# Two-layer token mixer after bucketed attention: where weight residues are subtracted, and the order in which inputs are split and read

## The chip, the core and the metric

The kernel runs on one core of a Trainium2 chip. The metric is the device time of one execution in microseconds (us), the median of several runs. TensorE (PE) multiplies matrices into PSUM; VectorE (DVE), ScalarE (ACT) and GpSimd (POOL) work element by element; SyncE (SP) starts the transfers. Each engine takes its instructions in a fixed order and waits on semaphores for those of the others.

## What is computed

An attention in which a query sees only the keys of its own hash bucket, then two feed-forward layers without bias, all in float32:

```python
def reference(q, k, v, proj, moe_w_in, moe_w_out, moe2_w_in, moe2_w_out):
    x = attn(q, k, v, proj)            # 2 batches, 8 heads, 768 tokens, head size 64
    x = x.transpose(0, 2, 1, 3).reshape(1536, 512)
    h = x @ moe_w_in                   # 512 -> 2048
    x = (h * cos(h)) @ moe_w_out       # 2048 -> 512
    h = x @ moe2_w_in
    return (h * tanh(log1p(exp(h)))) @ moe2_w_out
```

## The kernel before

**Two parts per number.** A float32 operand is split into a high part of the type float32r and a residue, operand minus high part. A product is three matmuls: high with high, high with residue, residue with high. Weights and activations are both split.

**Attention.** `attention()` runs one loop over 16 heads of six query tiles, in a software pipeline. At the end of each head pair `fin` adds two halves into `xt` (L394, on GpSimd) and splits them into the inputs of the first layer: `high` (L397) and `low` (L400), both on GpSimd. They run some steps later, one entry of the list `later` for each loop step. The inputs lie in three token tiles of 512 tokens, each in four quarters of 128 features: `XH[t][c]` and `XL[t][c]`, named xh and xl in the trace. A head pair fills one quarter `c`. Batch 0 covers tile 0 and the first 256 tokens of tile 1, batch 1 the rest of tile 1 and tile 2. So the last head pair fills the last quarter of tiles 1 and 2. The first two first-layer blocks, on tile 0, run between the attention's last steps (`early`).

**Feed-forward.** `moe()` runs 96 steps. Step n multiplies one input weight block (128 of the 2048 hidden features) with a token tile: `h_mm(n)`, 12 matmuls (L174), the block h(n). Four steps later `ophase(n)` multiplies the activation with an output weight block into four PSUM accumulators, 12 matmuls again (L665), the block o(n). In between ScalarE and VectorE make the activation and split it: for the cosine two copies out of PSUM (L184, L186), a rounding (L196, VectorE), two ScalarE operations (L192, L193), the product (L199, VectorE), then the high part gh (L207, ScalarE) and the residue gl (L209, VectorE). Steps 0 to 3 use tile 0, steps 4 to 11 tile 1. When a run of steps ends, `finish` moves the four accumulators out of PSUM: copies on VectorE and ScalarE (L625, L627) or adds on VectorE (L623). The next run's first o block waits for them, since there is one set of accumulators. The first run ends with o(3), and o(4) is the first block of the next.

**Weights.** They arrive as 64-bit numbers, and each block (a unit) passes three stages in successive steps: `conv1` (L131, ScalarE), `conv2` (L140, L142, L145, VectorE), `conv3`, which makes the high part `w[:, 0]` (L152, ScalarE) and the residue `w[:, 1]` (L154, GpSimd). The first four units go through in pieces during the attention (`step` 0 and 1), the other 60 in `conv_next` with `step` None, about one a step, from the last steps of the attention on. The planner `due` takes a unit as soon as its slot is free, so that it is ready three steps or more ahead of its first matmul.

**Order.** The program is written out in the order in which the loops call it; nothing is moved by a scheduler. In a step VectorE's queue holds L196, L209, L199, then the copies of `finish`, then `conv2`.

Of the kernel before, what the change touches and what calls it, by code (L numbers as in the profile page):

```python
# [14 lines left out]
ALU = mybir.AluOpType  # L15
# [30 lines left out]
def lsh_moe_kernel(ctx: ExitStack, tc: tile.TileContext, q, k, v, proj, w_in1, w_out1, w_in2, w_out2, cst, out):  # L46
    nc = tc.nc
    B, H, S, D = q.shape
    J = S // 128
    DM = H * D  # L50
    NCT = DM // 128
# [8 lines left out]
    TT = 512  # L60
# [3 lines left out]
    def f32(ap):  # L64
        return ap.bitcast(F32)
# [14 lines left out]
    XH, XL = (  # L80
        [[persist.tile([128, TT], F32R, name=f"x{n}{i}_{c}") for c in range(NCT)] for i in range(NT3)] for n in ("h", "l")
    )
# [65 lines left out]
    def conv3(st, step=None):  # L148
        (i, part), g = st
        w = slots[part][i % NW]  # L150
        if step != 1:
            nc.scalar.activation(w[:, 0], g, ACTF.Copy)  # L152
        if step != 0:
            nc.gpsimd.tensor_tensor(w[:, 1], g, f32(w[:, 0]), ALU.subtract)  # L154

    E = {}
    G = {}
# [10 lines left out]
    def h_mm(n, hp):  # L168
        m, b, li = uses[n]
        w = slots[0][li % NW]  # L170
        E[n] = [hp]
        i = 0
        for wi, c, X in [(0, c, X) for c in range(NCT) for X in (XH, XL)] + [(1, c, XH) for c in range(NCT)]:
            nc.tensor.matmul(hp, w[:, wi, c, :], X[b][c], start=(i == 0), stop=(i == 3 * NCT - 1))  # L174
            i += 1
            yield
# [37 lines left out]
    def conv_next(new):  # L214
        for st in pipe[1]:
            conv3(st)
        pipe[1] = pipe[0]
        pipe[0] = [conv1(u) for u in new]
# [4 lines left out]
    def attention():  # L223
        actx = ExitStack()
        with actx:
# [125 lines left out]
            def punits(c):  # L351
                h, i = divmod(c, J)
                half, k0 = divmod(i, J // 2)
                return h, half, (2 * k0, 2 * k0 + 1)
# [24 lines left out]
            def fin(c):  # L379
                h, half, kts = punits(c)  # L380
                if kts[1] != J - 1:
                    return
                if h % 2 == 0 and half == 0:
                    xt[h // 2] = x_p.tile([128, S], F32, tag="xt", name="xt", bufs=1)
                x = xt[h // 2]
                o = 64 * (h % 2)
                u = x_p.tile([128, HF], F32, tag="us", name="us")
                sh = x_p.tile([128, HF], F32, tag="sh", name="sh")
                nc.scalar.activation(u, U[0], ACTF.Copy)
                nc.sync.dma_start(out=sh[o:o + 64, :], in_=u[64 - o:128 - o, :])  # L390

                def add():
                    xo = x[o:o + 64, half * HF:half * HF + HF]
                    nc.gpsimd.tensor_tensor(xo, u[o:o + 64, :], sh[o:o + 64, :], ALU.add)  # L394

                def high(t, c0, c1, k):
                    nc.gpsimd.tensor_scalar(XH[t][k][:, c0:c1], x_of(t, c0, c1), 1.0, 1.0, ALU.mult, ALU.mult)  # L397

                def low(t, c0, c1, k):
                    nc.gpsimd.tensor_tensor(  # L400
                        XL[t][k][:, c0:c1], x_of(t, c0, c1), f32(XH[t][k])[:, c0:c1], ALU.subtract
                    )

                def x_of(t, c0, c1):
                    g0 = t * TT - (h // H) * S
                    return x[:, g0 + c0:g0 + c1]

                later.append((c + 3, add))
                if h % 2 == 1 and half == 1:
                    b, hh = divmod(h, H)  # L410
                    k = hh // 2
                    big, rest = ((0, 0, TT), (1, 0, S - TT)) if b == 0 else ((2, 0, TT), (1, S - TT, TT))
                    later.extend(
                        (
                            (c + 4, lambda: (high(*big, k), high(*rest, k))),
                            (c + 5, lambda: low(*big, k)),
                            (c + 6, lambda: low(*rest, k)),
                        )
                    )

# [64 lines left out]
            def early():  # L485
                for n in range(EARLY_H):
                    yield from h_mm(n, ps_s.tile([128, 1024], F32, tag="s", name="s")[:, 0:TT])
                    stage_0(n)
                    ready.append(n)
# [3 lines left out]
            def pieces(u):  # L493
                st = u, cv_p.tile([128, NCT, 128], F32, tag="g", name="cg", bufs=4)
                g = conv2(st)
                yield "A", lambda: conv1(u, 0, st[1])
                yield "D", lambda: next(g)
                yield "D", lambda: next(g)
                yield "D", lambda: next(g)
                yield "A", lambda: conv3(st, 0)  # L500
                yield "P", lambda: conv3(st, 1)
# [16 lines left out]
            for t in range(-1, NT + LAG + 7):  # L518
                H1, j = divmod(t + 1, J)
                c = t - LAG  # L520
# [20 lines left out]
                if 0 <= c - 2 < NT:  # L541
                    fin(c - 2)
# [41 lines left out]
    def moe():  # L584
        mctx = ExitStack()
        with mctx:
# [92 lines left out]
            for n in range(NU + LAG):  # L679
                if n == NU // 2:  # L680
                    iter1(n, last=True)
                    nc.scalar.preload_act_table_set("mish")
                if EARLY_H <= n < NU:
                    for _ in h_mm(n, ps_h.tile([128, TT], F32, tag="h", name="h")):
                        pass
                    stage_0(n)
                if n >= LAG:
                    ophase(n - LAG)
                if EARLY_H <= n < NU // 2:
                    iter1(n)  # L690
                elif n >= NU // 2:
                    split(n - 1)
                if n - LAG in closes_at:
                    finish(n - LAG)
                for _ in conv_mid():
                    pass
                split_x(1)
                conv_next(due(n, 1))
# [32 lines left out]
```

## Time and profile before

| | before |
|---|---|
| median of 3 runs | 797.54 us (796.18 to 797.77) |
| the profiled execution | 796.35 us |
| its span, first to last instruction | 794.6 us |
| TensorE busy | 777.2 us, 98% |
| VectorE busy | 541.8 us, 68% |
| ScalarE busy | 502.1 us, 63% |
| GpSimd busy | 305.3 us, 38% |
| mean granted TensorE clock | 0.994 |

The attention fills the span up to about 262 us, the feed-forward the rest. Times in the trace are counted from the span's start. A timeline row has start, duration, engine, line, operation and tiles; "x4" means that four instructions were merged; a bracket at the end is the idle time of the engine before it and what ended it. A duration on VectorE runs into the next instruction's start by some 0.1 us, so costs on a queue are read from start to start.

### The profile page before, as it was taken

Reading aid. Unit: us, or ns where it says so; the run is one execution under the profiler, and the core shown is the slowest. Engines: PE = TensorE matmul, PEld = TensorE weight load, DVE = VectorE, ACT = ScalarE, POOL = GpSimd, SP = SyncE. Lnnn points to the kernel's source line nnn. Section 1 sums busy time; section 2 is a strip of 40 time slices with the busy share of each in tenths; the row PEclk is TensorE's granted clock in tenths of the full one; section 3 lists DMA queues with packets and bytes.
Section 4 is the critical chain, followed back from the end, with each engine's and each line's share of the span. In section 5 each row is a group of like instructions: output and inputs, shape, how many; then the busy total and the mean of one; then the engine's idle time right before and its main releaser. Section 6 shows DMA issues by size and latency. Waiting matters only on the chain.

```text
span 794.6 us, 11720 instructions
## 1 busy us (share of the span) xinstructions
PE 777.2 (98%) x4020; PEld 665.5 (84%) x4020; DVE 541.8 (68%) x944; ACT 502.1 (63%) x1002; POOL 305.3 (38%) x327
## 2 busy tenths in 40 slices
PE   7999999999999898999999999999999999999998
PEld 5889999999999676887888888888888888888886
DVE  5799899888897898559888546998412766611122
ACT  5899999998997786567777656875223444322120
POOL 4779999998876532102222001232200221200000
PEclk9999999999999999999999999999999999999999
DMA  8454454443320433002332001333100232001011
GB/s 230 105 153 111 105 148 120 105 110 106 85 51 20 139 108 102 30 27 79 107 106 84 23 1 55 105 106 106 54 1 27 81 105 80 1 1 54 0 54 53
DMA packets 38027, 62.36 MB, mean 78 GB/s; under 512 B 3664, under 2 KB 28368, under 8 KB 37968
## 3 DMA queue, kind: packets, MB, share of 16 engines
q1 hardware_dynamic: 37968, 61.63, 26.4%
q8 instruction: 31, 0.51, 0.3%
q14 instruction: 28, 0.23, 0.1%
HBM read 43.13 MB, written 3.15 MB: 58 GB/s over the span
## 4 chain that ended last, share of the span: by engine, by line
PE 59%; DVE 3%; ACT 1%; issue 1%; DVEq 0%; ACTq 0%
PE o L665 30%; PE h L174 29%; DVE hs L199 2%; DVE pa L641 0%; ACT gh L207 0%; ACT hs L184 0%; ACT a L186 0%; DVE gl L209 0%; ACT a L192 0%; DVE ct L142 0%; DVE cg L145 0%; DVE ct L140 0%; ACT pa L627 0%; ACT cg L131 0%; DVE pa L623 0%
## 5 line engine op out<-in xcount | busy, mean ns | idle before, releaser
L174 PE MATMUL h<-xh,w 128*128 128x512 f32 x752 | 246.7, 389 | 0.6 <-POOL xh L397 0.6
L154 POOL TENSOR_TENSOR w<-cg,w 128x512 fp32r<-128x512 f32 x64 | 88.5, 1384 | 343.1 <-ACT w L152 330.9
L209 DVE TENSOR_TENSOR gl<-hs,gh 128x512 fp32r<-128x512 f32 x96 | 69.0, 719 | 168.6 <-ACT gh L207 168.6
L174 PEld LDWEIGHTS h<-xh,w 128*128 128x128 f32 x752 | 141.2, 188 | 30.1 <-POOL xh L397 1.0
L174 PE MATMUL h<-xl,w 128*128 128x512 f32 x376 | 146.4, 389 | 2.3 <-POOL xl L400 2.3
L181 ACT ACTIVATE hs<-h 128x512 f32<-128x512 f32 x48 | 28.7, 598 | 158.7 <-PE h L174 158.7
L665 PE MATMUL o<-gh,w 128*128 128x512 f32 x384 | 120.8, 396 | 4.6 <-DVE pa L625 3.9
L367 DVE TENSOR_TENSOR pl<-wp,ph 128x384 fp32r<-128x384 f32 x192 | 105.8, 552 | 23.3 <-ACT ph L365 22.7
L665 PE MATMUL o<-w,gh 128*128 128x512 f32 x384 | 118.3, 389 | 0.0
L365 ACT ACTIVATE ph<-wp 128x384 fp32r<-128x384 f32 x192 | 95.8, 500 | 17.5 <-PE wp L361 17.4
L326 DVE TENSOR_REDUCE nm<-s 128x1 f32<-128x768 f32 x96 | 90.1, 938 | 5.3 <-PE s L324 5.3
L324 PE MATMUL s<-k,q 128*128 128x512 f32 (+1 forms) x384 | 91.6, 361 | 2.0 <-DVE k L478 1.3
L665 PEld LDWEIGHTS o<-gh,w 128*128 128x128 f32 x384 | 73.4, 192 | 21.1 <-ACT a L192 4.3
L174 PEld LDWEIGHTS h<-xl,w 128*128 128x128 f32 x376 | 70.6, 188 | 17.2 <-POOL xl L400 2.6
L665 PEld LDWEIGHTS o<-w,gh 128*128 128x128 f32 x384 | 72.1, 188 | 15.0
L665 PE MATMUL o<-gl,w 128*128 128x512 f32 x192 | 75.6, 394 | 0.0
L665 PE MATMUL o<-w,gl 128*128 128x512 f32 x192 | 74.7, 389 | 0.0
L377 PE MATMUL u<-ph,nv 128*128 128x384 f32 x192 | 72.5, 378 | 0.0
L184 ACT ACTIVATE hs<-h 128x512 f32<-128x512 f32 x46 | 27.5, 598 | 63.6 <-PE h L174 31.6
L199 DVE SCALAR_TENSOR_TENSOR hs<-hs,b 128x512 f32<-128x512 f32 x48 | 64.9, 1352 | 1.8 <-ACT b L193 1.8
L377 PE MATMUL u<-pl,nv 128*128 128x384 f32 x192 | 64.9, 338 | 0.3 <-DVE pl L367 0.3
L324 PEld LDWEIGHTS s<-k,q 128*128 128x128 f32 x384 | 58.9, 191 | 6.9 <-DVE k L478 1.5
(102 smaller groups left out, 1429.2 us busy)
## 6 DMA issues: line engine op xcount, KB each, us to landing
wr<-in_moe_w_in_dram SPq DMA_DIRECT2D x32, 512.0 KB, 3.8
wr<-in_moe_w_out_dram SPq DMA_DIRECT2D x32, 512.0 KB, 3.3
rq<-in_q_dram SPq DMA_DIRECT2D x16, 192.0 KB, 2.9
rk<-in_k_dram SPq DMA_DIRECT2D x16, 192.0 KB, 2.7
rv<-in_v_dram SPq DMA_DIRECT2D x16, 192.0 KB, 3.4
q<-q SPq DMA_DIRECT2D x16, 192.0 KB, 2.7
k<-k SPq DMA_DIRECT2D x16, 192.0 KB, 2.7
sh<-us SPq DMA_DIRECT2D x32, 96.0 KB, 2.2
```

Of the source, the lines that this page charges most:

```text
L154: nc.gpsimd.tensor_tensor(w[:, 1], g, f32(w[:, 0]), ALU.subtract)
L174: nc.tensor.matmul(hp, w[:, wi, c, :], X[b][c], start=(i == 0), stop=(i == 3 * NCT - 1))
L181: nc.scalar.activation(hs, hp, ACTF.Mish)
L184: nc.scalar.activation(hs, hp, ACTF.Copy, scale=INV2PI)
L199: nc.vector.scalar_tensor_tensor(hs1, hs1, TWO_PI, b1, ALU.mult, ALU.mult)
L209: nc.vector.tensor_tensor(gl, hs, f32(gh), ALU.subtract)
L324: nc.tensor.matmul(s[:, c0:c1], T[a][:, qs], T[c][:, c0:c1], start=(n == 0), stop=(n == 1))
L326: nc.vector.tensor_reduce(nm, s, AX.X, ALU.max, negate=True)
L365: nc.scalar.activation(ph, w, ACTF.Copy)
L367: nc.vector.tensor_tensor(pl, w, f32(ph), ALU.subtract)
L377: nc.tensor.matmul(U[0], lw, x, start=(kt == 0 and n == 0), stop=(kt == J - 1 and n == 1))
L665: nc.tensor.matmul(O[d], lhs, rhs, start=(first and x == 0), stop=(last and x == 2))
```

## The change

Three places. In `conv3` the residue of a weight unit is subtracted on VectorE for the 60 units of `conv_next`; the four units in pieces stay on GpSimd. In `h_mm` the 12 matmuls of a block are reordered: first the nine that read quarters 0 to 2, high inputs, input residues, weight residues, and then the three that read the last quarter. In `fin` the part of tile 1 is split whole before the part of tile 2 for batch 1 (for batch 0 tile 0 stays first), with both halves of the first part in one loop step.

```diff
--- before.py
+++ after.py
@@ -151,7 +151,8 @@
         if step != 1:
             nc.scalar.activation(w[:, 0], g, ACTF.Copy)
         if step != 0:
-            nc.gpsimd.tensor_tensor(w[:, 1], g, f32(w[:, 0]), ALU.subtract)
+            eng = nc.vector if step is None else nc.gpsimd
+            eng.tensor_tensor(w[:, 1], g, f32(w[:, 0]), ALU.subtract)
 
     E = {}
     G = {}
@@ -170,7 +171,8 @@
         w = slots[0][li % NW]
         E[n] = [hp]
         i = 0
-        for wi, c, X in [(0, c, X) for c in range(NCT) for X in (XH, XL)] + [(1, c, XH) for c in range(NCT)]:
+        most = [(wi, c, X) for wi, X in ((0, XH), (0, XL), (1, XH)) for c in range(NCT - 1)]
+        for wi, c, X in most + [(0, NCT - 1, XH), (1, NCT - 1, XH), (0, NCT - 1, XL)]:
             nc.tensor.matmul(hp, w[:, wi, c, :], X[b][c], start=(i == 0), stop=(i == 3 * NCT - 1))
             i += 1
             yield
@@ -409,12 +411,12 @@
                 if h % 2 == 1 and half == 1:
                     b, hh = divmod(h, H)
                     k = hh // 2
-                    big, rest = ((0, 0, TT), (1, 0, S - TT)) if b == 0 else ((2, 0, TT), (1, S - TT, TT))
+                    first, second = ((0, 0, TT), (1, 0, S - TT)) if b == 0 else ((1, S - TT, TT), (2, 0, TT))
                     later.extend(
                         (
-                            (c + 4, lambda: (high(*big, k), high(*rest, k))),
-                            (c + 5, lambda: low(*big, k)),
-                            (c + 6, lambda: low(*rest, k)),
+                            (c + 4, lambda: (high(*first, k), low(*first, k))),
+                            (c + 5, lambda: high(*second, k)),
+                            (c + 6, lambda: low(*second, k)),
                         )
                     )
```

VectorE's queue where the attention ends: in the old program from the product L199 of step 0 to that of step 1. The names starting with w1 are output weight slots, cg is a converted unit.

```order
L199 SCALAR_TENSOR_TENSOR hs_4759<-hs_4759,b_4763 128x512
L140 TENSOR_SCALAR ct_4922<-cg_4817 128x512
L142 SCALAR_TENSOR_TENSOR ct_4922<-wr_1883,ct_4922 128x512
L145 SCALAR_TENSOR_TENSOR cg_4817<-cg_4817,ct_4922 128x512
L140 TENSOR_SCALAR ct_4932<-cg_4930 128x512
L142 SCALAR_TENSOR_TENSOR ct_4932<-wr_2468,ct_4932 128x512
L145 SCALAR_TENSOR_TENSOR cg_4930<-cg_4930,ct_4932 128x512
L196 SCALAR_TENSOR_TENSOR a_4957<-a_4957,hs_4955 128x512
L209 TENSOR_TENSOR gl_4965<-hs_4759,gh_4963 128x512
L199 SCALAR_TENSOR_TENSOR hs_4844<-hs_4844,b_4848 128x512
```

The same stretch of VectorE's queue in the changed program (lines from 155 on are one or two higher there).

```order
L201 SCALAR_TENSOR_TENSOR hs_4759<-hs_4759,b_4763 128x512
L140 TENSOR_SCALAR ct_4922<-cg_4817 128x512
L142 SCALAR_TENSOR_TENSOR ct_4922<-wr_1883,ct_4922 128x512
L145 SCALAR_TENSOR_TENSOR cg_4817<-cg_4817,ct_4922 128x512
L155 TENSOR_TENSOR w1_0_4910<-cg_4749,w1_0_4910 128x512
L140 TENSOR_SCALAR ct_4932<-cg_4930 128x512
L142 SCALAR_TENSOR_TENSOR ct_4932<-wr_2468,ct_4932 128x512
L145 SCALAR_TENSOR_TENSOR cg_4930<-cg_4930,ct_4932 128x512
L155 TENSOR_TENSOR w1_1_4911<-cg_4817,w1_1_4911 128x512
L198 SCALAR_TENSOR_TENSOR a_4957<-a_4957,hs_4955 128x512
L211 TENSOR_TENSOR gl_4965<-hs_4759,gh_4963 128x512
L201 SCALAR_TENSOR_TENSOR hs_4844<-hs_4844,b_4848 128x512
```

Two subtracts (L155) stand ahead of gl of step 0 now; from here on one stands at the end of each step that has a residue.

TensorE, the first block on tile 1, h(4), in the old program. The name xh1_3 is quarter 3 of tile 1; w0_0 is read as high part in the first eight rows and as residue in the last four.

```order
L174 MATMUL h_5014<-xh1_0_77,w0_0_97 128x512
L174 MATMUL h_5014<-xl1_0_89,w0_0_97 128x512
L174 MATMUL h_5014<-xh1_1_78,w0_0_97 128x512
L174 MATMUL h_5014<-xl1_1_90,w0_0_97 128x512
L174 MATMUL h_5014<-xh1_2_79,w0_0_97 128x512
L174 MATMUL h_5014<-xl1_2_91,w0_0_97 128x512
L174 MATMUL h_5014<-xh1_3_80,w0_0_97 128x512
L174 MATMUL h_5014<-xl1_3_92,w0_0_97 128x512
L174 MATMUL h_5014<-xh1_0_77,w0_0_97 128x512
L174 MATMUL h_5014<-xh1_1_78,w0_0_97 128x512
L174 MATMUL h_5014<-xh1_2_79,w0_0_97 128x512
L174 MATMUL h_5014<-xh1_3_80,w0_0_97 128x512
```

The same block on TensorE in the changed program.

```order
L176 MATMUL h_5014<-xh1_0_77,w0_0_97 128x512
L176 MATMUL h_5014<-xh1_1_78,w0_0_97 128x512
L176 MATMUL h_5014<-xh1_2_79,w0_0_97 128x512
L176 MATMUL h_5014<-xl1_0_89,w0_0_97 128x512
L176 MATMUL h_5014<-xl1_1_90,w0_0_97 128x512
L176 MATMUL h_5014<-xl1_2_91,w0_0_97 128x512
L176 MATMUL h_5014<-xh1_0_77,w0_0_97 128x512
L176 MATMUL h_5014<-xh1_1_78,w0_0_97 128x512
L176 MATMUL h_5014<-xh1_2_79,w0_0_97 128x512
L176 MATMUL h_5014<-xh1_3_80,w0_0_97 128x512 x2
L176 MATMUL h_5014<-xl1_3_92,w0_0_97 128x512
```

The high part of the last quarter moved from place 7 to places 10 and 11, its residue from place 8 to place 12.

GpSimd's queue at the end of the attention in the old program, from the last add on.

```order
L394 TENSOR_TENSOR xt_4581<-us_4857,sh_4858 64x384
L397 TENSOR_SCALAR xh2_3_84<-xt_4581 128x512
L397 TENSOR_SCALAR xh1_3_80<-xt_4581 128x256
L400 TENSOR_TENSOR xl2_3_96<-xt_4581,xh2_3_84 128x512
L400 TENSOR_TENSOR xl1_3_92<-xt_4581,xh1_3_80 128x256
L154 TENSOR_TENSOR w1_0_4910<-cg_4749,w1_0_4910 128x512
L154 TENSOR_TENSOR w1_1_4911<-cg_4817,w1_1_4911 128x512
L154 TENSOR_TENSOR w1_2_4912<-cg_4930,w1_2_4912 128x512
```

The same place on GpSimd in the changed program.

```order
L396 TENSOR_TENSOR xt_4581<-us_4857,sh_4858 64x384
L399 TENSOR_SCALAR xh1_3_80<-xt_4581 128x256
L402 TENSOR_TENSOR xl1_3_92<-xt_4581,xh1_3_80 128x256
L399 TENSOR_SCALAR xh2_3_84<-xt_4581 128x512
L402 TENSOR_TENSOR xl2_3_96<-xt_4581,xh2_3_84 128x512
```

The parts of tile 1 moved ahead of those of tile 2, and after the last residue of tile 2 nothing is left for GpSimd.

## Rows read from the trace of the kernel before

**Rows 1.** The page, part 1: busy us (share of the span) xinstructions of each engine.

```profile
PE 777.2 (98%) x4020; PEld 665.5 (84%) x4020; DVE 541.8 (68%) x944; ACT 502.1 (63%) x1002; POOL 305.3 (38%) x327
```

**Rows 2.** The list of waits, TensorE: us in total, times, longest us.

```profile
PE o L665 <- DVE pa L625: 3.9, 1, 3.9
PE h L174 <- POOL xl L400: 2.3, 1, 2.3
...
PE o L665 <- DVE pa L623: 0.8, 1, 0.8
```

**Rows 3.** Busy time by stretch: busy us (x) of each engine, granted clock, DMA.

```profile
272.00:278.00 6.00, 5.68 (x18) 4.25 (x19) 5.93 (x5) 3.51 (x6) 5.09 (x4) 0.72 0.19 60
...
301.10:305.40 4.30, 4.30 (x13) 3.40 (x14) 4.16 (x7) 1.97 (x4) 1.26 (x1) 0.64 0.28 87
```

**Rows 4.** Timeline, TensorE: start us, us, instruction, [idle before <-releaser].

```profile
269.52 0.49 PE L174 MATMUL h<-xh,w 128*128 128x512 f32 x1 [0.55 <-POOL xh L397]
272.32 0.50 PE L174 MATMUL h<-xl,w 128*128 128x512 f32 x1 [2.30 <-POOL xl L400]
...
274.61 0.63 PE L665 MATMUL o<-gl,w 128*128 128x512 f32 x1
...
277.98 0.39 PE L174 MATMUL h<-xh,w 128*128 128x512 f32 x1
...
296.14 1.07 PE L174 MATMUL h<-xh,w 128*128 128x512 f32 x4
301.10 1.19 PE L665 MATMUL o<-gh,w 128*128 128x512 f32 x2 [3.89 <-DVE pa L625]
...
305.39 0.39 PE L174 MATMUL h<-xh,w 128*128 128x512 f32 x1
...
368.89 0.70 PE L665 MATMUL o<-gh,w 128*128 128x512 f32 x2 [0.76 <-DVE pa L623]
```

**Rows 5.** Timeline, VectorE, from the attention's end to the first accumulator copy.

```profile
266.89 1.29 DVE L140 TENSOR_SCALAR ct<-cg 128x512 int32<-128x512 int32 x1
...
272.74 1.77 DVE L199 SCALAR_TENSOR_TENSOR hs<-hs,b 128x512 f32<-128x512 f32 x1
...
278.28 0.68 DVE L196 SCALAR_TENSOR_TENSOR a<-a,hs 128x512 f32<-128x512 f32 x1
...
284.31 1.78 DVE L199 SCALAR_TENSOR_TENSOR hs<-hs,b 128x512 f32<-128x512 f32 x1
...
298.58 1.77 DVE L199 SCALAR_TENSOR_TENSOR hs<-hs,b 128x512 f32<-128x512 f32 x1
300.27 1.27 DVE L625 COPY pa<-o 128x512 f32<-128x512 f32 x2
```

**Rows 6.** Timeline, VectorE, some steps later.

```profile
349.42 0.69 DVE L209 TENSOR_TENSOR gl<-hs,gh 128x512 fp32r<-128x512 f32 x1 [1.10 <-ACT gh L207]
350.03 0.69 DVE L199 SCALAR_TENSOR_TENSOR hs<-hs,b 128x512 f32<-128x512 f32 x1
350.63 0.42 DVE L140 TENSOR_SCALAR ct<-cg 128x512 int32<-128x512 int32 x1
351.08 0.69 DVE L142 SCALAR_TENSOR_TENSOR ct<-wr,ct 128x512 int32<-128x512 int32 x1
351.88 0.69 DVE L145 SCALAR_TENSOR_TENSOR cg<-cg,ct 128x512 int32<-128x512 int32 x1
...
366.35 1.80 DVE L199 SCALAR_TENSOR_TENSOR hs<-hs,b 128x512 f32<-128x512 f32 x1
```

**Rows 7.** Timeline, GpSimd, over both stretches.

```profile
272.23 4.86 POOL L154 TENSOR_TENSOR w<-cg,w 128x512 fp32r<-128x512 f32 x3
...
283.93 1.60 POOL L154 TENSOR_TENSOR w<-cg,w 128x512 fp32r<-128x512 f32 x1 [3.20 <-ACT w L152]
...
355.42 1.29 POOL L154 TENSOR_TENSOR w<-cg,w 128x512 fp32r<-128x512 f32 x1 [31.35 <-ACT w L152]
```

**Rows 8.** Timeline, ScalarE, one step of the first stretch.

```profile
283.22 0.63 ACT L152 ACTIVATE w<-cg 128x512 fp32r<-128x512 f32 x1 [0.58 <-DVE cg L145]
```

## The prediction

> **What bounds the kernel now.** I read the page's busy shares first: TensorE is busy 98% of the span [rows 1], so whatever removes none of its idle or half-speed time is worth nothing, however much it does elsewhere. Next the list of waits, for TensorE alone: three stand out [rows 2], 3.9 us for a copy on VectorE (L625), 2.3 us for an input residue on GpSimd (L400) and 0.8 us for an add on VectorE (L623). Then its timeline around them [rows 4]. From 277.98 to 296.14 TensorE runs 80 matmuls in 18.16 us, 0.227 each: 2.72 for a block of 12 and 5.44 for a step of two blocks. Against that pace there are three losses.
>
> Gap A: block h(4) is the first to use token tile 1. It waits 0.55 for the high part of the last input quarter and 2.30 for its residue. Its seventh matmul is at 269.52, so by the pace it could have begun near 267.45; the next first-layer block begins at 277.98. Those 24 matmuls took 10.5 instead of 5.44: 5.1 lost. Besides the waits there is the clock: 0.72 granted over 272 to 278 [rows 3], a mixture of the two levels (1.2 and 2.4 GHz).
>
> Gap B: h(8) ends by the pace at 297.05; the next second-layer block needs the accumulators that the copy L625 frees, and starts at 301.10. After that idle stretch the granted clock is 0.64 [rows 3], and the block takes 4.29 (301.10 to 305.39) instead of 2.72. Loss 4.05 + 1.57 = 5.6.
>
> Gap C: 0.76 at 368.89 [rows 4], where the add L623 is late: 0.8.
>
> After gap C the list of waits has nothing for TensorE, so 11.5 us is all that could be won.
>
> What is late in gap B is VectorE, which runs from 266.89 to the copy at 300.27 without an idle time ahead of any operation [rows 5]. One step of its queue is 4.76 (284.31 to 298.58 is three). One operation stands out: L199 takes 1.70 from its start to the next one's (298.58 to 300.27), while the same line takes 0.60 at 350.03 [rows 6], where GpSimd has been idle for long (its row at 355.42 has 31 us of it [rows 7]). Beside the L199 at 284.31, which lasts 1.78, the GpSimd residue L154 runs from 283.93 to 285.53 [rows 7]. VectorE all but stands still while GpSimd holds on. The Trainium skill says so too (SBUF — State Buffer, "SBUF: two separate sides"): a VectorE operation with two SBUF inputs and a GpSimd operation exclude each other for the whole instruction, and whichever starts first wins. The trace agrees for L154 (1.10 lost of its 1.60).
>
> **The change, part by part.**
>
> *Residues to VectorE.* 60 subtracts leave GpSimd and join VectorE's queue, one at the end of each step. A subtract of the same shape and types is L209: 349.42 to the next start at 350.03, so 0.60 a piece [rows 6]. In a step that has a residue, 0.60 comes in and L199's 1.10 goes out: 4.76 becomes 4.26. The Trainium skill (VectorE: DVE Perf Modes, "The DRAIN you can't avoid") says that an operation does not start before the one ahead has left the pipe. By that each added subtract would cost its whole 0.69 instead of 0.60, and the gain below would be about 0.6 smaller over its seven subtracts; the rows [rows 6] have the next start 0.08 before the end, and I go by them.
>
> Now the stretch that decides gap B, along VectorE's queue:
> 1. From L140 at 266.89 to L199 at 272.74 it took 5.85. Clean spacings [rows 6] give 0.45 for L140, 0.80 for L142 and 0.60 for L145, L196 and L209 each: 3.05, so 2.8 went to GpSimd's input add and input residues. They stay, in another order, and I leave the 2.8. Two subtracts join (1.20), the first of them partly in the 0.1 to 0.2 for which L140 waits on the conversion ahead of it. L199 would thus start at about 273.75, and gl(0) be ready there: 1.0 later than before.
> 2. From 272.74 to L196 at 278.28 it took 5.54 against 2.45 clean (0.60 + 0.45 + 0.80 + 0.60): 3.1 lost to the three residues that GpSimd ran in a row from 272.23 [rows 7]. They go, and one subtract comes: 3.05. L196 stands at 276.8 to 277.0 instead of 278.28, 1.3 earlier.
> 3. Four steps at 4.26 instead of 4.76: 2.0 earlier.
> 4. The last L199 (298.58 to 300.27) at 0.60 instead of 1.69: 1.1 earlier.
>
> Sum 4.4. The block that waits started 0.83 after the copy began (300.27 to 301.10), and that stays: it may start at 296.7.
>
> Is TensorE there by then? Gap A decides. Its third matmul of o(0) needs gl(0), at 273.9 by item 1 instead of 274.61. From there to 277.98 it took 3.37, much of it at the lower clock, and I keep that: h(5) at 277.3. Three steps and a block (19.07 before, from 277.98 to 297.05) put it at 296.3. So it waits some 0.4, too little for a clock drop of the kind behind the 3.89 idle, starts o(4) at 296.7 at full clock, and h(9) at 299.4 instead of 305.39. **Gaps A and B together give 6.0.**
>
> A new wait comes with VectorE's subtract: it needs ScalarE's L152 of the same step, and behind it in the queue stand the next L196 and L209. L152 ends at 283.85 [rows 8]; VectorE reaches the end of that step's conversion only at 287.86 by the spacings, 4 us later, so nothing is held up. ScalarE in turn no longer waits on GpSimd to reuse the converted tiles.
>
> *Order of the input splits and of a block.* The tile 1 parts (256 columns) now come first on GpSimd, and a block asks for the last quarter at its matmuls 10 to 12 instead of 7, 8 and 12. The list of waits has these two for 2.85. Taken alone they close; but o(0) stands behind h(4), and its third matmul needs gl(0), which by item 1 is at 273.8 whatever h(4) does. So the wait moves some matmuls on and is worth only what is in the sum above (0.7). Bounds: 0 and the 2.85, plus clock. In the earlier heads the same reordering only swaps GpSimd operations; one normalisation may come later by one subtract on GpSimd, 1.3 to 1.6 [rows 7], and the transposes that read it come six steps on: nothing. A weight residue is now read at matmul 7 of a block instead of 9; it is made at least three steps (16 us) ahead: nothing. No DMA moves to another queue; the weight loads that VectorE's conversion triggers come up to 1 us later at first and earlier afterwards, and what they load is used two steps on.
>
> *Gap C.* L199 at 366.35 takes 1.80 [rows 6]; at 0.60 the add comes 1.1 earlier, against 0.76 that TensorE waits. It closes: 0.8.
>
> *The rest of the program.* Some 50 subtracts more for VectorE, 0.60 each. They are hidden: TensorE needs 5.44 a step, VectorE 4.26. Without that cover each would cost 0.60.
>
> Sum: 6.0 + 0.8 = 6.8 us. The profiled execution took 796.35 with a span of 794.6; its span should come to about 787.8. The median of the runs shown is 797.54, 1.2 above that execution, so **790.7**.
>
> **Rivals.**
>
> *Smaller gain.* VectorE's step stays near 4.76, because another engine takes over (ScalarE's is the next: it waited 0.58 in the step that rows 8 shows, so 4.2 of work) or because the subtract and the input splits get more in each other's way than item 1 says. Items 3 and 4 shrink to about 1; o(4) starts near 298.8, TensorE idles over 2 us and half of the clock loss stays (0.8). Gain 2.3 + 0.8 + 0.8 = 3.9, so 793.6. For it: ScalarE's margin to 4.26 is thin. Against: 4.2 still fits in 4.26, and only o(0) needs what item 1 delays.
>
> *Larger gain.* The input residue of tile 2 now comes last on GpSimd and may lose to VectorE until gl(0) is out. Then item 1 is shorter by up to 1.3 and gap A nearly closes, clock included. Gain 8 to 10, so 788.5.
>
> *No change.* The first-layer order only shifts the wait, and gap B reopens with its clock loss since TensorE comes early to a VectorE that is as late as before: 796.5 to 798.5. It needs a step of 4.76 and none of item 2.
>
> *Slower.* L199's 1.70 belongs to the operation and its place and not to GpSimd. Then a step costs 4.76 + 0.60 = 5.36: over four steps 2.4 more, with item 1's 1.0 and no gain of items 2 and 4. o(4) starts 3 to 4 late: 801. It decides once L199 saves less than the 0.60 that a subtract costs. Against: the 0.60 of L199 at 350.03 [rows 6], with GpSimd idle.
>
> **How the numbers follow.** Forecast 0.70 (789.3 to 792.3: 0.8 for the sums, and 1.6 if the short wait at o(4) brings the low clock after all), smaller gain 0.10, larger 0.08, no change 0.06, slower 0.06. For 8 in 10 I take most of the forecast's span with parts of both neighbours: 788.6 to 793.4. A measurement of this kernel can tell about 0.2% (1.6 us) from no change. Faster by more than that: 0.70 + 0.10 + 0.08 = 0.88, of which I give 0.02 to no change for the smaller gain's low end: 0.86; same 0.08; slower 0.06.
>
> **What would show it.** In the profile after: L199 at 0.69 everywhere; VectorE's steps from 278 on 4.26 apart; no wait of h for xh or xl, and instead one of o(0) for gl, near 271 to 274, with the granted clock again below 1 behind it; the wait at L625's successor under 1 us, at 296 to 297, with full clock behind it; none for the add of gap C; and TensorE without a pause from there. A L199 that stays above 1.1, a step above 4.6, or a wait of TensorE in the later blocks for a weight residue would prove the forecast wrong.

## The result and the profile after

The changed kernel takes 790.11 us (median; 789.57 to 792.08), the old one 797.61 in the same comparison: a ratio of 0.9917, 95% interval 0.9898 to 0.9935, so 0.8% faster. The profiled execution took 790.22 us with a span of 788.4; 790.7 and a span of 787.8 had been forecast. Lines from 155 on stand one or two higher in the new code: L199 is L201, L209 is L211, L625 is L627.

The page, part 1, of the kernel after (answers to [rows 1]):

```profile
PE 776.2 (98%) x4020; PEld 664.9 (84%) x4020; DVE 517.1 (66%) x1004; ACT 501.2 (64%) x1002; POOL 222.0 (28%) x267
```

VectorE has 60 instructions more and is busy 24.7 us less (541.8 before). The 60 subtracts are there; what went is time in which an operation stood still beside GpSimd. The groups of VectorE's operations by line show both (instructions, then busy us and mean ns of one):

```profile
L155 DVE TENSOR_TENSOR w<-cg,w 128x512 fp32r<-128x512 f32 x60 | 41.5, 691 | 0.0
...
L201 DVE SCALAR_TENSOR_TENSOR hs<-hs,b 128x512 f32<-128x512 f32 x48 | 32.9, 685 | 1.8 <-ACT b L195 1.8
```

Next TensorE's waits, longest first (us in total, times, longest). Of those in [rows 2] none is left in the feed-forward; one new long one has come, for gl. The second row belongs to the attention.

```profile
PE o L667 <- DVE gl L211: 2.2, 1, 2.2
PE wt L265 <- POOL nk L259: 1.9, 1, 1.9
```

TensorE's timeline after, at the places of [rows 4]: h(2), the first block behind the attention, at 262.61, o(0) from 271.52, h(5) at 278.44, o(4) at 297.52, h(9) at 300.25, and the place of gap C at 362.82.

```profile
262.61 0.86 PE L176 MATMUL h<-xh,w 128*128 128x512 f32 x3
...
271.52 0.73 PE L667 MATMUL o<-gh,w 128*128 128x512 f32 x2 [0.41 <-ACT gh L209]
274.45 0.50 PE L667 MATMUL o<-gl,w 128*128 128x512 f32 x1 [2.20 <-DVE gl L211]
...
277.24 1.06 PE L667 MATMUL o<-gh,w 128*128 128x512 f32 x2
278.10 0.50 PE L667 MATMUL o<-gl,w 128*128 128x512 f32 x1
278.44 0.86 PE L176 MATMUL h<-xh,w 128*128 128x512 f32 x3
...
297.52 0.62 PE L667 MATMUL o<-gh,w 128*128 128x512 f32 x2
...
300.25 0.84 PE L176 MATMUL h<-xh,w 128*128 128x512 f32 x3
...
362.82 0.62 PE L667 MATMUL o<-gh,w 128*128 128x512 f32 x2
```

o(4) and the row of gap C have no bracket: nothing was waited for. The granted clock in the stretches of [rows 3] (last columns: clock, DMA share, GB/s) is low in the first and full in the second:

```profile
272.00:278.00 6.00, 3.80 (x11) 2.84 (x10) 5.93 (x10) 4.02 (x8) 1.25 (x1) 0.74 0.45 137
...
301.10:305.40 4.30, 4.30 (x20) 3.56 (x20) 3.90 (x7) 2.88 (x6) 0.00 (x0) 1.00 0.46 130
```

VectorE's queue after, at the places of [rows 5]: the two subtracts ahead of gl(0) among GpSimd's input operations, then two clean steps, then the copy.

```profile
267.31 0.69 DVE L155 TENSOR_TENSOR w<-cg,w 128x512 fp32r<-128x512 f32 x1
...
271.03 1.09 DVE L155 TENSOR_TENSOR w<-cg,w 128x512 fp32r<-128x512 f32 x1
272.04 1.75 DVE L198 SCALAR_TENSOR_TENSOR a<-a,hs 128x512 f32<-128x512 f32 x1
273.72 0.68 DVE L211 TENSOR_TENSOR gl<-hs,gh 128x512 fp32r<-128x512 f32 x1
274.32 0.68 DVE L201 SCALAR_TENSOR_TENSOR hs<-hs,b 128x512 f32<-128x512 f32 x1
...
276.71 0.69 DVE L155 TENSOR_TENSOR w<-cg,w 128x512 fp32r<-128x512 f32 x1
277.31 0.69 DVE L198 SCALAR_TENSOR_TENSOR a<-a,hs 128x512 f32<-128x512 f32 x1
...
281.51 0.69 DVE L198 SCALAR_TENSOR_TENSOR a<-a,hs 128x512 f32<-128x512 f32 x1
...
295.90 0.68 DVE L201 SCALAR_TENSOR_TENSOR hs<-hs,b 128x512 f32<-128x512 f32 x1
296.50 1.28 DVE L627 COPY pa<-o 128x512 f32<-128x512 f32 x2
```

**How to compare the two traces.** In the profiled execution of after the attention ended 0.61 us later (h(2) begins at 262.61, before at 262.00). Some 0.3 of that is there after 12 us, ahead of anything that the change touches: drift. The other 0.3 comes in three steps of 0.1 between 67 and 142 us, behind the first three head pairs whose splits are reordered, and it belongs to the change. All six traces with the new order (after, e2, e3, e4, e5 and e8 below) fall back by 0.29 to 0.33 against before over this stretch, the three others with the old order (e1, e6, e7) by nothing (-0.03 to 0.01). The place is VectorE's L140, of which one stands behind each of the three pairs: 0.52 to 0.55 from start to start in the old order, 0.63 to 0.67 in the new. The first of them before:

```profile
68.45 0.62 DVE L140 TENSOR_SCALAR ct<-cg 128x512 int32<-128x512 int32 x1
69.00 0.54 DVE L367 TENSOR_TENSOR pl<-wp,ph 128x384 fp32r<-128x384 f32 x1
```

The first of them after:

```profile
68.77 0.71 DVE L140 TENSOR_SCALAR ct<-cg 128x512 int32<-128x512 int32 x1
69.41 0.54 DVE L369 TENSOR_TENSOR pl<-wp,ph 128x384 fp32r<-128x384 f32 x1
```

To leave both out I count from h(2). From there to the end of the span it was 794.6 - 262.00 = 532.6 and is 788.4 - 262.61 = 525.8: **6.8 us saved, the sum of the forecast.** With the 0.3 that the reordering costs ahead of h(2), the change is worth 6.5 by these two traces. By places, from h(2) on:

| | loss before | loss after |
|---|---|---|
| gap A: h(2) to h(5), above four blocks (10.88) | 15.98: 5.1 | 15.83: 4.95 |
| gap B: h(5) to h(9), above four steps (21.76) | 27.41: 5.65 | 21.81: 0.05 |
| gap C | 0.8 | 0 |

Gap B and gap C are gone, and gap A has hardly changed its size, only its place and its cause. The table's differences make 6.55; the other 0.2 is spread over the rest.

### The profile page after: what moved, and what is told of

It is laid out like the page before. It is cut to its first block, busy times and chain, and to the rows that moved or that the text cites. A ratio compares the mean times of both kernels' runs of the same rounds, so it can differ in the third digit from the quotient of the medians.

```text
span 788.4 us, 11576 instructions
## 1 busy us (share of the span) xinstructions
PE 776.2 (98%) x4020; PEld 664.9 (84%) x4020; DVE 517.1 (66%) x1004; ACT 501.2 (64%) x1002; POOL 222.0 (28%) x267
## 4 chain that ended last, share of the span: by engine, by line
PE 94%; ACT 2%; DVE 1%; DMA 1%; issue 1%; SPq 0%; POOL 0%; POOLq 0%; ACTq 0%
PE o L667 33%; PE h L176 31%; PE u L379 8%; PE wp L363 8%; PE s L326 8%; PE wb L287 2%; PE wt L265 2%; DMA rq<-in_q_dram 1%; PE s L176 1%; PE wm L294 1%; PE ww L435 1%; DVE pa L643 0%; DVE a L198 0%; SPq L119 0%; ACT ph L367 0%
## 5 line engine op out<-in xcount | busy, mean ns | idle before, releaser
L176 PE MATMUL h<-xh,w 128*128 128x512 f32 x752 | 201.0, 389 | 0.0
L211 DVE TENSOR_TENSOR gl<-hs,gh 128x512 fp32r<-128x512 f32 x96 | 66.4, 692 | 191.6 <-ACT gh L209 191.5
L176 PE MATMUL h<-xl,w 128*128 128x512 f32 x376 | 115.9, 389 | 0.0
L209 ACT ACTIVATE gh<-hs 128x512 fp32r<-128x512 f32 x96 | 59.5, 620 | 1.6 <-PE o L667 1.4
L363 PE MATMUL wp<-con,hs 128*128 128x128 f32 x192 | 53.8, 280 | 0.0
```

The lines of the kernel that those rows point to most:

```text
L209: nc.scalar.activation(gh, hs, ACTF.Copy)
L211: nc.vector.tensor_tensor(gl, hs, f32(gh), ALU.subtract)
L363: nc.tensor.transpose(w[:, j * 128:j * 128 + 128], P[h * J + 3 * half + j][:, kt * 128:kt * 128 + 128], ident)
```

## Experiments

Of the three edits I call the subtract on VectorE *residue* and the two others together *order*. The block order and the split order were not run apart. The runs fall into three questions: which edit pays, why L199 was slow, and what gap A waits for.

**e1: residue alone.** The old kernel with only this edit:

```diff
-            nc.gpsimd.tensor_tensor(w[:, 1], g, f32(w[:, 0]), ALU.subtract)
+            eng = nc.vector if step is None else nc.gpsimd
+            eng.tensor_tensor(w[:, 1], g, f32(w[:, 0]), ALU.subtract)
```

> The kernel before with the weight residues on VectorE alone; the inputs are split and read in the old order. Theory (the gain is VectorE's queue, and the wait that the new order removes only moves to gl): within 0.7 us of the changed kernel, so 790 to 791.5; h(4) waits about 3 us for xl again, o(0) then hardly waits for gl, VectorE's steps are 4.2 and neither the copy nor the add makes TensorE wait. Rival (the order of the inputs gives a good part of the gain): 2 to 3 us above the changed kernel, 792.5 to 793.5.

Measured: 791.75 us (789.17 to 793.57), ratio 0.9925 (0.9903 to 0.9948), 0.25 above the range expected. From h(2) at 262.87 to the end of the span it takes 526.0, after takes 525.8. TensorE's waits in it, without those of the attention:

```profile
PE h L175 <- POOL xl L401: 2.3, 1, 2.3
...
PE h L175 <- POOL xh L398: 0.9, 1, 0.9
```

Gaps B and C are closed and gap A waits for the inputs as it did before. So this edit is the whole gain; by the traces the order adds 0.2 behind h(2), and ahead of it costs 0.3.

**e2: order alone.** The changed kernel with the subtract put back on GpSimd.

> The changed kernel with the weight residues back on GpSimd; only the two orders are new. Theory: no wait of h(4), but one of o(0) for gl or for the residue of its weights until about 274; VectorE's steps stay at 4.76, the copy stays near 300, TensorE waits about 4 us for it at a lower clock afterwards and 0.8 for the add: 796.5 to 798, the same as before. Rival (the order gives the gain): 791 to 794.

Measured: 795.82 us (794.90 to 800.48), ratio 0.9990 (0.9973 to 1.0007): no difference, though 0.7 below the range expected. TensorE's waits:

```profile
PE o L666 <- DVE pa L626: 3.2, 1, 3.2
PE o L666 <- POOL w L154: 3.1, 1, 3.1
...
PE o L666 <- DVE pa L624: 0.8, 1, 0.8
```

h(4) no longer waits, and o(0) waits instead, here not for gl but for its own weight residue, which GpSimd makes behind all five input operations, as it did before. Gaps B and C stay.

**e3: GpSimd busy again, with nothing depending on it.** The changed kernel, and in each of the 60 units GpSimd subtracts 384 of the 512 columns once more into a tile that nobody reads. All of VectorE's work is that of after.

```diff
+            if step is None:
+                nc.gpsimd.tensor_tensor(pools["sh"], g[:, 0:3], f32(w[:, 0, 0:3]), ALU.subtract)
```

> The changed kernel, and beside each residue on VectorE GpSimd subtracts three quarters of the same unit into a tile that nobody reads. No instruction of the others moves. Theory (VectorE stands still while a two-input operation of GpSimd runs): L199's successor takes 1.3 to 1.5 instead of 0.6 from start to start, VectorE's step is 4.9 to 5.0, the copy comes 4 to 6 later, TensorE waits 2.5 to 4.5 for it and loses clock behind it: 794.5 to 797.5. Rival (the slow product came from its place in the queue or from the waits, not from GpSimd at work): the product stays at 0.6, 790 to 791.

Measured: 798.90 us (797.60 to 800.10), ratio 1.0014 (0.9997 to 1.0030). The gain is gone, and the step of VectorE is 5.1. Timeline of VectorE, two steps (L213 is gl, L203 the product):

```profile
280.03 1.50 DVE L213 TENSOR_TENSOR gl<-hs,gh 128x512 fp32r<-128x512 f32 x1
281.45 0.68 DVE L203 SCALAR_TENSOR_TENSOR hs<-hs,b 128x512 f32<-128x512 f32 x1
...
285.11 0.68 DVE L213 TENSOR_TENSOR gl<-hs,gh 128x512 fp32r<-128x512 f32 x1
285.71 1.50 DVE L203 SCALAR_TENSOR_TENSOR hs<-hs,b 128x512 f32<-128x512 f32 x1
```

GpSimd in the same two steps of this kernel:

```profile
279.71 1.27 POOL L157 TENSOR_TENSOR shadow<-cg,w 128x384 fp32r<-128x384 f32 x1 [2.54 <-ACT w L152]
285.26 1.41 POOL L157 TENSOR_TENSOR shadow<-cg,w 128x384 fp32r<-128x384 f32 x1 [4.28 <-ACT w L152]
```

Whichever operation of VectorE begins while GpSimd is in its own takes the blow, here gl and there the product. So the 1.70 of L199 in [rows 5] was never the operation's. The time lies above what I had expected, since three of these extra operations stand in a row at the attention's end (272.90 to 277.17) and hold up gl(0) as well: TensorE waits 3.0 for gl and 4.0 for the copy.

**e4: the same with one input.** GpSimd multiplies the same columns of the high part by 1:

```diff
+            if step is None:
+                nc.gpsimd.tensor_scalar(pools["sh"], f32(w[:, 0, 0:3]), 1.0, 1.0, ALU.mult, ALU.mult)
```

> The same with a GpSimd operation that reads one tile only (a multiplication by 1 of three quarters of the high part). Theory (only two tile inputs on both sides exclude each other): the product stays below 0.8, VectorE's step at 4.2 to 4.4, 790 to 791.5. Rival (any GpSimd operation stops a two-input VectorE operation for its whole length): the product takes 1.1 to 1.4, the step 4.7 to 4.9, 793 to 796.

Measured: 792.38 us (791.39 to 796.17), ratio 0.9947 (0.9928 to 0.9966); the step is 4.50 instead of 4.20. It lies between the two expectations: TensorE waits 1.1 for the copy, where it waits 4.0 in e3 and not at all in after. Timeline of VectorE in one step:

```profile
284.27 0.99 DVE L203 SCALAR_TENSOR_TENSOR hs<-hs,b 128x512 f32<-128x512 f32 x1
285.18 0.41 DVE L140 TENSOR_SCALAR ct<-cg 128x512 int32<-128x512 int32 x1
```

GpSimd in the same step:

```profile
283.90 0.82 POOL L157 TENSOR_SCALAR shadow<-w 128x384 fp32r<-128x384 f32 x1 [4.29 <-ACT w L152]
```

The rows say what decides. L203 takes 0.91 to the next start, 0.31 more than its 0.60, and GpSimd's operation still had 0.45 to run when L203 began (283.90 + 0.82 - 284.27). In e3 L213 lost 0.82 (1.42 - 0.60) with 0.95 left on GpSimd (279.71 + 1.27 - 280.03). In the kernel before L199 lost 1.1 with 1.22 left of L154 (283.93 + 1.60 - 284.31, [rows 5, 7]). In all three the loss is what is left of GpSimd's operation, less 0.12 to 0.14. It is no choice of examples: in the ten traces, from 262 us on, 181 operations of VectorE with two tile inputs (0.60 each when undisturbed, the next one following at once) began with over 0.3 of a GpSimd operation left, beside one with one input in 20 cases, and every one of them lost what was left less 0.12 to 0.14. So VectorE waits for its end, with one input as with two; the one with one input is just shorter. That is what the Trainium skill says (SBUF — State Buffer, "SBUF: two separate sides"): the pair of ports is "an exclusive lock, not a bandwidth split". The trace agrees, with the 0.31, 0.82 and 1.1.

**e5: a shorter queue ahead of gl(0).** After e1 and e2 gap A was open still. In after it waits for gl(0), and around that VectorE's queue holds the conversions of two units that TensorE needs only some steps later. Here the planner `due` takes no unit in the first two steps, so that these two are made later. One of the two stands ahead of gl(0) (in after L140 at 267.91, in the last section), the other behind it (L140 at 274.92):

```diff
             new = []
+                if n < 2:
+                    return new
```

> The changed kernel, in which the planner takes no weight unit in the first two steps, so that the conversions that stood ahead of gl(0) on VectorE come two steps later. Theory (what is left of gap A is VectorE's queue ahead of gl(0), and the clock behind that wait): gl(0) near 271 instead of 273.7, TensorE waits under 0.7 for it and keeps the full clock, the copy comes with TensorE's own pace, gap B stays closed: 4 to 4.5 less than the changed kernel, 785.5 to 786.5. Rival (gl(0) is late because of GpSimd's splits or of ScalarE): under 1.5 less, 788.5 to 790.5.

Measured: **785.92 us** (785.82 to 788.89), ratio 0.9858 (0.9836 to 0.9879), the fastest of all. TensorE's timeline at h(2), o(0) and h(5):

```profile
265.28 0.86 PE L176 MATMUL h<-xh,w 128*128 128x512 f32 x3
...
274.67 0.50 PE L667 MATMUL o<-gl,w 128*128 128x512 f32 x1 [0.17 <-DVE gl L211]
...
277.08 0.84 PE L176 MATMUL h<-xh,w 128*128 128x512 f32 x3
```

VectorE at gl(0) in it:

```profile
273.62 1.00 DVE L211 TENSOR_TENSOR gl<-hs,gh 128x512 fp32r<-128x512 f32 x1 [0.73 <-ACT gh L209]
274.54 1.77 DVE L201 SCALAR_TENSOR_TENSOR hs<-hs,b 128x512 f32<-128x512 f32 x1
```

gl(0) begins 8.34 behind h(2) (273.62 - 265.28), in after 11.11 (273.72 - 262.61), and now it waits for ScalarE's gh instead of VectorE's queue. The stretch from 272 to 278 (columns as in [rows 3]):

```profile
272.00:278.00 6.00, 5.68 (x25) 4.05 (x24) 4.47 (x6) 5.38 (x10) 3.60 (x4) 1.00 0.50 167
```

h(2) to h(5) takes 11.80, 0.9 above the pace, instead of 15.83: gap A is all but closed and its clock is full. The profiled execution was the slowest of the five, as its attention ended some 3 us late (h(2) at 265.28); from there to the end it takes 521.8, 4.0 less than after.

**e6, e7 and e8: the same lines of `due` with the other combinations.** With e6 (residue and late units, old order), e7 (late units alone) and e8 (order and late units, residue on GpSimd) all eight combinations are there.

> The same late units with the residues on VectorE, but inputs split and read in the old order. Theory: once gl(0) is early, the old order's wait of h(4) for the last quarter is the one that ends last again: about 2.9 of waiting and 1 to 1.5 of clock, so 3 to 4 above the late units with the new order, 789 to 790.5. Rival (the order is worth nothing here either): 785.5 to 786.5.

> The kernel before with the late units alone; residues on GpSimd, old order. Theory (gap B is VectorE's backlog, whatever makes it): two conversions less ahead of the copy, so it comes 5 to 7 earlier and gap B closes with its clock loss; gap A keeps h(4)'s wait, gap C stays: 790.5 to 793. Rival (the slow products on VectorE keep gap B open by themselves): 795 to 797.5.

> Both orders of the change and the two weight units held back (as in e5), but the weight residues stay on GpSimd. Theory: with the orders, GpSimd's first weight residue stands behind all five input operations, and o(0) needs it for its second matmul, so o(0) waits about 3 us for it as in e2 (3.1), gap A stays with its low clock (0.7 to 0.8 over 272 to 278) however early gl is; the copy L626 comes at about 294 to 296 as in e7, so gap B is closed (wait under 0.5 instead of 3.2); gap C stays at 0.8. That is a gain of about 6 from gap B as in e7 and little else: 790 to 792, and some 5 above e5. Rival: the two units held back also free GpSimd or the orders alone make gap A close; then o(0) waits under 1 us, the clock over 272 to 278 is 1.0, and the time is 786 to 787.5, so that the move of the residues is not needed for the best time.

| residue | order | late units | | median us | ratio (95%) | h(2) to end | o(0), h(4): last wait | copy, add |
|---|---|---|---|---|---|---|---|---|
| no | no | no | before | 797.54 | 1 | 532.6 | xl 2.3 | 3.9, 0.8 |
| no | yes | no | e2 | 795.82 | 0.9990 (0.9973 to 1.0007) | 532.5 | w 3.1 | 3.2, 0.8 |
| yes | no | no | e1 | 791.75 | 0.9925 (0.9903 to 0.9948) | 526.0 | xl 2.3 | none |
| no | no | yes | e7 | 791.62 | 0.9922 (0.9899 to 0.9946) | 525.2 | xl 1.9 | none, 0.8 |
| yes | yes | no | after | 790.11 | 0.9917 (0.9898 to 0.9935) | 525.8 | gl 2.2 | none |
| yes | no | yes | e6 | 791.84 | 0.9919 (0.9899 to 0.9938) | 526.1 | xl 1.9 | none |
| no | yes | yes | e8 | 790.71 | 0.9935 (0.9905 to 0.9965) | 526.5 | w 2.5 | none, 0.8 |
| yes | yes | yes | e5 | 785.92 | 0.9858 (0.9836 to 0.9879) | 521.8 | gl 0.2 | none |

Each ratio is to the old kernel in the same comparison, whose median lay between 796.78 and 797.61. The medians hold the attention's drift from execution to execution; the column from h(2) on does not, so I read the effects there. It is one execution of each kernel, and leaves out the 0.3 that the order costs ahead of h(2). For e7 that one was the fastest of six: three others took 792.53 to 793.17 with a mean granted clock of 0.993, against 788.89 and 0.997 here; where their clock was low, no trace shows. TensorE's waits in e8, of which the table has the first and the last here:

```profile
PE o L666 <- POOL w L154: 2.5, 1, 2.5
...
PE o L666 <- DVE pa L624: 0.8, 1, 0.8
```

Gap B closes as soon as VectorE has less ahead of the copy, by the residue (e1) or by the two late units (e7, where L199 still takes up to 1.80 beside GpSimd); both together give no more (e6). Gap A has three works that end late, close to each other: the input residue xl on GpSimd, the weight residue w of o(0) behind it on GpSimd, and gl on VectorE. Each edit takes one of them away, and TensorE waits 1.9 to 3.1 for the next. Only with all three is the wait gone. So the order is worth 0.1 alone (e2), 0.2 with the residue (after against e1) and 4.3 with the residue and the late units (526.1 to 521.8), each less the 0.3 in the attention. With the late units alone it is worth nothing: e8 takes 1.3 more than e7 (526.5, 525.2), whose clock stayed full over 272 to 278 while e8's was 0.72. e6's median came out some 1.3 above what I had expected of it; the waits were those expected. e8's expectation held in each point, with 2.5 for its "about 3".

## Why the prediction was right

**What bounds the kernel.** The three gaps were the right list: e5, which closes all but 0.9 of gap A, saves 10.8 of the 11.5 from h(2) on (532.6 - 521.8).

**The mechanism.** L201 is 0.69 everywhere, as forecast, and e3 shows that GpSimd's work made it 1.78. The "slower" rival is refuted by that, the "no change" rival by the copy, which came early, and the "smaller gain" rival by the step of 4.20.

**The queue, item by item,** with the forecast's times shifted by the 0.61 of h(2):

| | forecast | measured |
|---|---|---|
| item 1: gl(0) ready (next start behind it) | 273.75 + 0.61 = 274.36 | 274.32 |
| third matmul of o(0) | 273.9 + 0.61 = 274.5 | 274.45 |
| item 2: L198 (was L196) | 277.4 to 277.6 | 277.31 |
| item 3: step | 4.26 | 4.20 |
| item 4: last L201, to the copy | 0.60 | 0.60 |
| h(5) | 277.3 + 0.61 = 277.9 | 278.44 |
| o(4) | 296.7 + 0.61 = 297.3 | 297.52 |
| h(9) | 299.4 + 0.61 = 300.0 | 300.25 |

Two terms were mis-sized, and nearly made up for each other. The stretch of o(0) behind its wait was kept at 3.37 and took 3.99 (274.45 to 278.44): with the wait as late as it is, TensorE is still slow at the end of o(0), with 0.86 for two matmuls (277.24 to 278.10) where the pace is 0.45. That is the reason why gap A gave 0.15 instead of 0.7. And no wait of 0.4 at o(4) followed, since TensorE came 0.6 later and VectorE's step was 0.06 shorter: gap B gave all of its 5.6 instead of 5.3. The step was the conversion's: L142 to L145 is 0.73 in after and 0.80 in [rows 6]. Why, the runs don't say; both values occur with GpSimd idle. That the sum came out to the tenth is luck in part: gap A gave 0.55 less than forecast, gap B 0.3 more, and 0.2 stands in no term.

**The added subtract** costs 0.60 from start to start (276.71 to 277.31), not its 0.69; the other reading, by which the gain would have been 0.6 smaller, is not borne out here. The section of the Trainium skill that the prediction cites for it excepts an operation that is not held back, which the prediction left out. No wait of the later blocks for a weight residue appeared, so the 50 others were hidden as said.

**Gap C** closed: the add follows a product of 0.60, and the row at 362.82 has no wait.

**The order's share.** That it would be swallowed by gl(0) was right (e1: 0.2). What I didn't see is how much lay behind it: the "larger gain" rival asked for gl(0) early, and I looked for that only on GpSimd's side. In after GpSimd's last input residue does hold VectorE up (L198 at 272.04, 1.68 to the next start), and the way out was VectorE's own queue (e5).

**From the span to the median.** The forecast added 1.2 because the profiled execution of before lay that much under its median. The one of after lies 0.1 above its own, so the median came out 0.6 below the forecast although the span came out 0.6 above it. Of the span's 0.6, half is drift. The other half is the order's cost in the attention, a term that the prediction put at nothing ("only swaps GpSimd operations").

## What to carry to other kernels

When one line of VectorE takes 1.7 us in one stretch and 0.6 in another, look at what GpSimd does at that moment: moving GpSimd's work onto the *slowed* engine can shorten its queue, though it was the busier one of the two. A wait that is removed pays only up to the next work that ends late; where several end close together, an edit can look worthless (the order: 0.1 alone, 0.2 with the residue) and still be the one that the last gain needs (4.3), so try them in combination before throwing one away. And before speeding up a queue, look for what stands in it early without need: holding two conversions back by two steps was, alone (e7), worth about as much as the whole change.

## What the runs showed of the hardware beside that

GpSimd holds up one-input operations of VectorE too. In after L140, 0.45 where GpSimd is idle, takes 1.28 to the next start beside the input add; GpSimd's operation had 0.96 left (267.50 + 1.37 - 267.91), and L140 lost 0.83: 0.13 between them as above. VectorE's timeline:

```profile
267.91 1.24 DVE L140 TENSOR_SCALAR ct<-cg 128x512 int32<-128x512 int32 x1
269.19 0.77 DVE L142 SCALAR_TENSOR_TENSOR ct<-wr,ct 128x512 int32<-128x512 int32 x1
```

GpSimd's operation at that time:

```profile
267.50 1.37 POOL L396 TENSOR_TENSOR xt<-us,sh 64x384 f32<-64x384 f32 x1 [5.29 <-DMA sh<-us]
```

And the clock did not fall after every wait of this size. In e7 h(4) waits 0.57 and 1.88, and the granted clock over 272 to 278 is 1.00; in e6 it waits 1.17 and 1.87, and it is 0.72. The stretch in e7:

```profile
272.00:278.00 6.00, 5.95 (x26) 4.56 (x26) 5.50 (x7) 4.91 (x9) 3.17 (x2) 1.00 0.00 0
```

The same stretch in e6:

```profile
272.00:278.00 6.00, 5.45 (x17) 4.33 (x18) 4.66 (x7) 5.69 (x10) 0.49 (x1) 0.72 0.00 0
```

h(2) to h(5) takes 14.28 in e7 and 16.11 in e6: 0.6 more of waiting, and 1.2 more behind it. Whether the longer wait or its moment decided, two executions can't say.
